# Moving one transpose of a fused attention and SwiGLU kernel from the tensor engine to the DMA engines

## The chip, the core and the metric

The kernel runs on one core of a Trainium2 chip. The metric is the device time of one execution in microseconds (us). One first run of the kernel before took 747.17 us. A profile's span is one execution as the trace sees it and is 1.5 to 1.8 us shorter than the time.

In profile lines, PE is the matrix engine (PEld its weight loads), DVE the vector engine, ACT the scalar engine, POOL and SP the two engines that issue the DMAs looked at here. SPq is SP's DMA queue: its time is that which one issue holds the queue. A DMA has landed when its data are complete for whoever waits; the time to landing counts from the start of its issue. A bracket such as [0.77 <-PE ps L441] gives how long the engine was idle before, and what ended that. `L466` is a line of that kernel's own file. Line numbers shift between kernels, so the text says what each one is.

## The reference, cut to what matters

```python
# attention, window of 64 keys, causal; B = H = 8, S = 576, D = 64
scores = where(0 <= i - j < 64, q @ k.T / 8, -1e9)
attn   = softmax(scores) @ v
x = attn.transpose(0, 2, 1, 3).reshape(4608, 512)
# feed-forward
g   = x @ w_gate;  val = x @ w_val            # 512 -> 1536
out = (g * sigmoid(g) * val) @ w_out          # 1536 -> 512, float32
```

## The kernel before

The 4608 tokens are 36 chunks of 128, and nine groups of four chunks. Attention works by chunk: `T` transposes q and k on PE, `Sx` makes scores, `AV` the weighted sum of v. DVE normalises that into `xb` (128 tokens x 512 features, bf16), in two halves. The feed-forward needs x with the features on the partitions, so `X` transposes `xb` into a quarter of `xT`. `F` then works on a whole group (512 columns of `xT`), `O` on one chunk of the group before. A helper records each operation with what it reads and writes; each engine runs its list in order and waits on semaphores.

```python
    def load_v(self, n):
        ...                                   # POOL: va <- v, cast to bf16
        g.op("sp", lambda e: e.dma_start(vb[64:128], va[0:64]), reads=lo, writes=[("vb", i, 1)], dma=True)
        if n + 1 < NCH:
            ...
            g.op("sp", lambda e: e.dma_start(vb2[0:64], va[64:128]), reads=hi, writes=[("vb", i2, 0)], dma=True)

    def T(self, n):
        ...                                   # PE: 4 transposes of kn, 4 of qn, into one PSUM bank
        g.op("dve", lambda e: e.tensor_copy(kd, tb[:, 0]), reads=[bk], writes=[("kT", n, p) for p in range(4)] + [(bk, "k")])
        g.op("act", lambda e: e.activation(qz[0:64, :, 0, :], tb[0:64, 1], ACTF.Copy),
             reads=[bk, (bk, "k")], writes=[("qz", iz, p, 0) for p in range(4)])
        g.op("dve", lambda e: e.tensor_copy(qz[64:128, :, 1, :], tb[64:128, 1]), reads=[bk], writes=[...])

    def X(self, n, eng="dve"):
        ...
        def pe(e):
            for c in range(4):
                r = e.transpose(tb[:, c, :], xb[:, 128 * c:128 * c + 128], self.ident[:, :])
            return r
        g.op("pe", pe, reads=["ident", ("xb", ix, 0), ("xb", ix, 1)], writes=[bk])
        ...
            g.op("dve", lambda e: e.tensor_copy(xo, tb), reads=[bk], writes=[("xT", it, u)])

    def F(self, c, f):
        ...
        xk = [("xT", it, u) for u in range(4)]          # all four quarters
        g.op("pe", mm(G, self.Wg), reads=xk + [("Wg", f)], writes=[gk])
        ...

    # the steady part of build()
        for c in range(1, NFC):                          # groups
            for u in range(4):
                n = 4 * c + u + 4                        # the chunk whose attention runs beside group c
                live = n < NCH
                load(n + 4)
                self.F(c, 3 * u)
                if live:
                    self.AV(n, 0)
                    if n + 1 < NCH:
                        self.Sx(n + 1, 0)
                self.F(c, 3 * u + 1)
                if live:
                    self.AV(n, 1)
                    if n + 1 < NCH:
                        self.Sx(n + 1, 1)
                if c > 1:
                    self.O(c - 1, u)
                if live and c > 1:
                    self.X(n)
                self.F(c, 3 * u + 2)
                ...
                if n + 2 < NCH:
                    self.T(n + 2)
```

The softmax here doesn't subtract the row's maximum and nothing guards it: scores larger than these inputs give would overflow.

Of the kernel before, what the change touches and what calls it, by code (L numbers as in the profile page):

```python
# [10 lines left out]
NCH = T // 128  # L11
# [138 lines left out]
class _Kernel:  # L150
# [165 lines left out]
            else:  # L316
                g.op("dve", lambda e, d=d, a=a: e.tensor_copy(d, a), reads=[bk], writes=zk)

    def load_v(self, n):
        g = self.g  # L320
        i = n % self.NV
        va = self.va[i]
        parts = list(self.segs(128 * n, 128))
        for j, (r, b, s, L) in enumerate(parts):
            d = va[r:r + L, :, 0:64]
            a = self.v[b, :, s:s + L, :].rearrange("h p d -> p h d")
            ks = [("va", i, j)] if len(parts) > 1 else [("va", i, 0), ("va", i, 1)]
            g.op("pool", lambda e, d=d, a=a: e.dma_start(d, a), writes=ks, dma=True)  # L328
        vb = self.vb[i]
        lo = [("va", i, 0), ("va", i)]  # L330
        hi = [("va", i, 0 if len(parts) == 1 else 1), ("va", i)]
        g.op("sp", lambda e: e.dma_start(vb[64:128], va[0:64]), reads=lo, writes=[("vb", i, 1)], dma=True)
        if n + 1 < NCH:
            i2 = (n + 1) % self.NV
            vb2 = self.vb[i2]
            g.op("sp", lambda e: e.dma_start(vb2[0:64], va[64:128]), reads=hi, writes=[("vb", i2, 0)], dma=True)
# [95 lines left out]
    def X(self, n, eng="dve"):  # L432
# [16 lines left out]
        else:  # L449
            g.op("act", lambda e: e.activation(xo, tb, ACTF.Copy), reads=[bk], writes=[("xT", it, u)])  # L450

    def F(self, c, f):
        g = self.g
        it, ih = c % self.NX, c % self.NH
        xT, hT = self.xT[it], self.hT[ih]
        i = self.n_s % self.NS
        self.n_s += 1
        sig, uu = self.sig[i], self.uu[i]
        xk = [("xT", it, u) for u in range(4)]
        G, gk = self.bank("f")  # L460
        V, vk = self.bank("f")

        def mm(bank, W):
            def pe(e):
                for kk in range(NK):
                    r = e.matmul(bank[:, :], W[:, kk, f * 128:f * 128 + 128], xT[:, kk, :],  # L466
                                 start=(kk == 0), stop=(kk == NK - 1))
                return r
            return pe

        g.op("pe", mm(G, self.Wg), reads=xk + [("Wg", f)], writes=[gk])
        g.op("act", lambda e: e.activation(sig[:, :], G[:, :], ACTF.Tanh, scale=0.5), reads=[gk], writes=[("sig", i)])  # L472
        g.op("pe", mm(V, self.Wv), reads=xk + [("Wv", f)], writes=[vk])
        g.op("dve", lambda e: e.scalar_tensor_tensor(uu[:, :], sig[:, :], 1.0, G[:, :], ALU.add, ALU.mult),  # L474
             reads=[("sig", i), gk], writes=[("uu", i)])
        g.op("dve", lambda e: e.scalar_tensor_tensor(hT[:, f, :], uu[:, :], 0.5, V[:, :], ALU.mult, ALU.mult),  # L476
             reads=[("uu", i), vk], writes=[("hT", ih, f)])
# [28 lines left out]
    def build(self):  # L506
        W = lambda a, b: (self.load_w("g", a, b), self.load_w("v", a, b))

        def load(n):
            if n < NCH:  # L510
                self.load_qk(n)
                self.load_v(n)

        self.first_loads()
        self.init()
        self.load_v(0)
        self.init_pool_a()
        self.load_v(1)
        self.init_pool_b()
        self.load_v(2)  # L520
        self.load_v(3)
        W(0, 1)
        W(1, 2)
        for f in range(2, 12, 2):
            W(f, f + 2)

        self.banks("a", [5, 6, 7, 4, 0, 1, 2, 3])
        self.first_casts(0)
        self.init_pt()
        self.first_T(0)  # L530
        self.first_T(1)
        self.first_casts(1)
        self.init_nmask()
        self.Sx(0, 0, True)
        self.Sx(1, 0, True)
        self.first_T(2)
        self.Sx(2, 0, True)
        self.first_T(3)
        self.Sx(3, 0, True)
        for n in range(4):  # L540
            self.Sx(n, 1, True)
            self.AV(n, 0)
        for n in range(4):
            self.AV(n, 1)
            if n > 0:
                self.X(n - 1, "act")
        self.X(3, "act")
        self.banks("a", [5, 6, 7])
        self.init_va(4)
        load(4)  # L550
        load(5)
        self.load_wo(0, 6)
        self.load_wo(6, 12)

        for f in range(6):
            self.F(0, f)
        self.T(4)
        self.F(0, 6)
        self.Sx(4, 0)
        self.F(0, 7)  # L560
        self.Sx(4, 1)
        self.T(5)
        load(6)
        self.F(0, 8)
        self.AV(4, 0)
        self.Sx(5, 0)
        self.F(0, 9)
        self.AV(4, 1)
        self.Sx(5, 1)
        load(7)  # L570
        self.F(0, 10)
        self.X(4)
        self.AV(5, 0)
        self.F(0, 11)
        self.AV(5, 1)
        self.T(6)
        load(8)
        self.O(0, 0)
        self.X(5)
        self.Sx(6, 0)  # L580
        self.T(7)
        load(9)
        self.Sx(6, 1)
        self.O(0, 1)
        self.AV(6, 0)
        self.Sx(7, 0)
        self.AV(6, 1)
        self.Sx(7, 1)
        self.T(8)
        self.O(0, 2)  # L590
        self.X(6)
        self.AV(7, 0)
        self.Sx(8, 0)
        self.AV(7, 1)
        self.Sx(8, 1)
        self.T(9)
        self.O(0, 3)
        self.X(7)
        load(10)
        load(11)  # L600
        for c in range(1, NFC):
            for u in range(4):
                n = 4 * c + u + 4
                live = n < NCH
                load(n + 4)
                self.F(c, 3 * u)
                if live:
                    self.AV(n, 0)
# [4 lines that stand above are left out]
                    self.AV(n, 1)  # L613
                    if n + 1 < NCH:
                        self.Sx(n + 1, 1)
                if c > 1:
                    self.O(c - 1, u)
                if live and c > 1:
                    self.X(n)
                self.F(c, 3 * u + 2)  # L620
                if live and c == 1:
                    self.X(n)
                if n + 2 < NCH:
                    self.T(n + 2)
        self.banks("o", [0, 1, 2, 3])
        for u in range(4):
            self.O(NFC - 1, u)
        self.g.emit()
# [42 lines left out]
```

## Time and profile before

| | |
|---|---|
| time | 376.6 us |
| PE busy, 160 to 220 us | 59.76 of 60 us |
| one chunk in the steady part | 9.64 us |
| `X` of one chunk, time that it holds PE | 0.22 us |
| `X` on DVE (one copy) | 0.42 us |

The busy line of the page of the kernel before: busy us, share of the span, instructions.

```profile
PE 352.3 (94%) x2624; PEld 192.0 (51%) x2624; DVE 254.6 (68%) x550; ACT 152.3 (41%) x260; POOL 107.5 (29%) x136
```

The chain of waits of the kernel before, over one chunk, without the short pieces of `AV`: start, us, what. L489 is `O`, L441 `X`, L466 `F`, L360 `T`, L389 `Sx`.

```profile
200.17 2.59 PE ps L489 x12
202.76 0.22 PE ps L441 x4
202.98 1.73 PE ps L466 x8
204.71 0.45 PE ps L360 x8
205.16 1.73 PE ps L466 x8
...
207.13 0.28 PE ps L389 x4
207.41 1.73 PE ps L466 x8
...
209.41 0.40 PE ps L389 x4
```

The next `O` begins at 209.81. All but 0.03 us of it is PE's, so what shortens PE's list shortens the kernel. `X` is 0.22 us of 9.64. Note also that `Sx`, the same four matmuls, takes 0.28 us once and 0.40 us once; this comes back below.

What the DVE and PE timelines of the kernel before show at the end of a chunk: the second half of `xb` (L429), the copy of `X` (L448), and `T` (L360).

```profile
211.13 0.43 DVE L429 TENSOR_TENSOR xb<-ps,rc 128x256 bf16<-128x256 f32 x1
212.66 0.42 DVE L448 COPY xT<-ps 128x512 bf16<-128x512 bf16 x1 [0.77 <-PE ps L441]
214.18 0.39 PE L360 MATMUL ps<-ident,kn 128*128 128x128 bf16 x4
```

Between `xb` complete (211.56) and the first `F` of the next chunk (214.63) lie 3.07 us, and 2.85 us once `X` is gone from PE. For the last chunk of a group that is the room which a slower transpose has (2.6 us at the last group, where no `T` runs).

The windows view of the kernel before: window, length, busy us of PE, PEld, DVE, ACT and POOL (with instructions), PE's clock, DMA share (over 1 where packets queue), GB/s.

```profile
205.20:211.50 6.30, 6.27 (x49) 3.39 (x48) 5.42 (x13) 2.86 (x5) 2.63 (x3) 1.00 1.05 79
211.50:214.00 2.50, 2.50 (x17) 1.23 (x15) 0.81 (x3) 1.08 (x2) 0.00 (x0) 1.00 0.08 22
```

The loads of q, k and v keep the DMA engines occupied for about 6 of every 9.6 us. Just when `xb` is complete they are nearly idle (0.08).

### The profile page before, as it was taken

What the parts mean: (1) busy time and instruction counts of PE and PEld (TensorE: products, weight loads), DVE (VectorE), ACT (ScalarE), POOL (GpSimd) and SP (SyncE); (2) the same over time, 40 slices, a digit from 0 to 9 for tenths busy, and PEclk for the clock granted to TensorE, in tenths of its full rate; (3) what the DMA queues carried; (4) which work ended last, traced back from release to release, by engine and by line L of the source; (5) the groups of instructions that cost most, each with busy time, mean ns of one, the idle gap of its engine ahead of it and who ended that gap; (6) DMA issues with size and microseconds to landing.
All of it is one profiled execution on the core that took longest, in us unless ns stands there. A gap on an engine that the chain in (4) does not pass through costs nothing.

```text
span 375.1 us, 6635 instructions
## 1 busy us (share of the span) xinstructions
PE 352.3 (94%) x2624; PEld 192.0 (51%) x2624; DVE 254.6 (68%) x550; ACT 152.3 (41%) x260; POOL 107.5 (29%) x136
## 2 busy tenths in 40 slices
PE   1589999999899999999999999999999999999986
PEld 1564555555455555555555555555555555444432
DVE  6668876688867777777777777777777777655520
ACT  2553535435444444444444444444444444233311
POOL 8985525434222222322222222422220000000000
PEclk9999999999999999999999999999999999999999
DMA  9999999979957777777888787877771000010012
GB/s 236 202 201 175 204 173 205 169 47 91 84 71 85 86 86 87 82 88 87 90 87 89 78 94 86 86 83 77 78 82 37 30 29 30 28 58 28 28 38 104
DMA packets 126158, 35.61 MB, mean 95 GB/s; under 512 B 108272, under 2 KB 121520, under 8 KB 126128
## 3 DMA queue, kind: packets, MB, share of 16 engines
q0 software_dynamic: 113152, 17.83, 64.3%
q1 hardware_dynamic: 11920, 16.31, 13.5%
q10 hardware_dynamic: 1056, 1.05, 0.9%
q8 instruction: 21, 0.34, 0.4%
q14 instruction: 9, 0.07, 0.1%
HBM read 37.75 MB, written 9.44 MB: 126 GB/s over the span
## 4 chain that ended last, share of the span: by engine, by line
PE 81%; DVE 13%; ACT 3%; DMA 2%; issue 1%
PE ps L466 41%; PE ps L489 25%; PE ps L389 5%; DVE hT L476 4%; DVE uu L474 4%; PE ps L360 3%; PE ps L441 2%; PE ps L420 2%; PE ps L419 2%; DVE xb L429 2%; DMA f<-in_q_dram 2%; ACT sig L472 1%; DVE pt L407 1%; ACT qz L366 1%; PE ps L302 1%
## 5 line engine op out<-in xcount | busy, mean ns | idle before, releaser
L474 DVE SCALAR_TENSOR_TENSOR uu<-sig,ps 128x512 bf16<-128x512 bf16 x108 | 74.1, 686 | 65.1 <-ACT sig L472 65.1
L466 PE MATMUL ps<-xT,Wg 128*128 128x512 bf16 x432 | 111.0, 380 | 2.4 <-DVE xT L448 1.7
L466 PE MATMUL ps<-xT,Wv 128*128 128x512 bf16 x432 | 110.9, 379 | 0.0
L489 PE MATMUL ps<-Wo,hT 128*128 128x512 bf16 x432 | 98.7, 380 | 2.1 <-DVE hT L476 2.1
L472 ACT ACTIVATE sig<-ps 128x512 bf16<-128x512 f32 x108 | 64.0, 592 | 43.4 <-PE ps L466 43.4
L277 POOL DMA_DIRECT2D qn<-in_q_dram x36 | 30.4, 847 | 164.2 <-PE ps L360 161.3
L476 DVE SCALAR_TENSOR_TENSOR hT<-uu,ps 128x512 bf16<-128x512 bf16 x108 | 74.2, 687 | 3.7
L466 PEld LDWEIGHTS ps<-xT,Wv 128*128 128x128 bf16 x432 | 42.2, 98 | 51.0
L489 PEld LDWEIGHTS ps<-Wo,hT 128*128 128x128 bf16 x432 | 40.9, 98 | 46.9 <-DVE hT L476 2.7
L401 ACT ACTIVATE pt<-ps 128x512 bf16<-128x512 f32 x72 | 42.9, 596 | 33.2 <-PE ps L389 30.5
L466 PEld LDWEIGHTS ps<-xT,Wg 128*128 128x128 bf16 x432 | 38.2, 98 | 32.6 <-DVE xT L448 2.0
L494 ACT ACTIVATE ost<-ps 128x512 f32<-128x512 f32 x36 | 21.5, 597 | 74.8 <-PE ps L489 74.8
L366 ACT ACTIVATE qz<-ps 64x512 bf16<-64x512 bf16 x32 | 18.9, 590 | 57.8 <-DVE kT L365 57.8
L328 POOL DMA_DIRECT2D va<-in_v_dram x40 | 34.7, 875 | 1.3 <-DVE wup L226 0.8
L389 PE MATMUL ps<-qz,kT 128*128 128x128 bf16 x288 | 30.8, 225 | 2.0 <-ACT qz L366 0.4
L429 DVE TENSOR_TENSOR xb<-ps,rc 128x256 bf16<-128x256 f32 x72 | 30.6, 425 | 2.5
L277 POOL DMA_DIRECT2D kn<-in_k_dram x36 | 30.7, 858 | 1.2 <-DMA Wv<-in_moe_w_val_dram 0.8
L448 DVE COPY xT<-ps 128x512 bf16<-128x512 bf16 x32 | 13.6, 423 | 24.1 <-PE ps L441 24.1
L407 DVE TENSOR_TENSOR pt<-pt,mask 128x512 bf16<-128x512 bf16 x64 | 26.6, 416 | 1.5 <-ACT pt L401 1.4
L419 PE MATMUL ps<-vb,pt 128*128 128x65 bf16 x288 | 26.9, 194 | 0.1
L420 PE MATMUL ps<-va,pt 128*128 128x65 bf16 x288 | 27.0, 194 | 0.0
L419 PEld LDWEIGHTS ps<-vb,pt 128*128 128x128 bf16 x288 | 22.6, 98 | 7.3 <-DVE xT L448 0.2
(44 smaller groups left out, 198.6 us busy)
## 6 DMA issues: line engine op xcount, KB each, us to landing
out_dram<-ost SPq DMA_DIRECT2D x36, 256.0 KB, 2.0
vb<-va SPq DMA_DIRECT2D x71, 80.0 KB, 2.1
va<-in_v_dram POOLq DMA_DIRECT2D x32, 128.0 KB, 4.5
qn<-in_q_dram POOLq DMA_DIRECT2D x28, 128.0 KB, 3.4
kn<-in_k_dram POOLq DMA_DIRECT2D x28, 128.0 KB, 4.4
Wo<-in_moe_w_out_dram POOLq DMA_DIRECT2D x2, 768.0 KB, 19.2
Wg<-in_moe_w_gate_dram POOLq DMA_DIRECT2D x5, 256.0 KB, 12.7
Wv<-in_moe_w_val_dram POOLq DMA_DIRECT2D x5, 256.0 KB, 13.3
```

The lines of the kernel that those rows point to most:

```text
L277: self.g.op("pool", lambda e, d=d, a=a: e.dma_start(d, a), writes=ks, dma=True)
L328: g.op("pool", lambda e, d=d, a=a: e.dma_start(d, a), writes=ks, dma=True)
L389: r = e.matmul(sv[:, w, c], self.kT[:, pr, k0:k0 + 128], qz[:, pr, :, 64 * w:64 * w + 64], start=not bias, stop=True)
L401: g.op("act", lambda e: e.activation(po, si, ACTF.Exp, scale=SCALE), reads=[bk], writes=[pk])
L419: e.matmul(av[:, j, :], pt[:, h, 0:128], vb[:, h, 0:65], start=True, stop=False)
L420: r = e.matmul(av[:, j, :], pt[:, h, 64:192], va[:, h, 0:65], start=False, stop=True)
L429: g.op("dve", lambda e: e.tensor_tensor(xo, av[:, :, 0:64], rb, ALU.mult), reads=[bk, ("rc", ir)], writes=[("xb", ix, half)])
L466: r = e.matmul(bank[:, :], W[:, kk, f * 128:f * 128 + 128], xT[:, kk, :], start=(kk == 0), stop=(kk == NK - 1))
L472: g.op("act", lambda e: e.activation(sig[:, :], G[:, :], ACTF.Tanh, scale=0.5), reads=[gk], writes=[("sig", i)])
L474: g.op("dve", lambda e: e.scalar_tensor_tensor(uu[:, :], sig[:, :], 1.0, G[:, :], ALU.add, ALU.mult), reads=[("sig", i), gk], writes=[("uu ...
L476: g.op("dve", lambda e: e.scalar_tensor_tensor(hT[:, f, :], uu[:, :], 0.5, V[:, :], ALU.mult, ALU.mult), reads=[("uu", i), vk], writes=[(" ...
L489: r = e.matmul(OB[:, :], hT[:, f, 128 * u:128 * u + 128], self.Wo[:, f, :], start=(f == 0), stop=(f == NF - 1))
```

## The change

The intent is to take the four transposes of `X` off PE, which bounds the kernel, and the copy off DVE. From group 3 on (chunks 12 to 35, 24 of 36) one DMA from SBUF to SBUF transposes `xb` into `xT`. The copies `vb <- va`, on the same SP queue, move from the load to behind that transpose.

```diff
+    def XD(self, n):
+        ix, it, u = n % 4, (n // 4) % self.NX, n % 4
+        xb = self.xb[ix]
+        xo = self.xT[it][:, :, 128 * u:128 * u + 128]
+        self.g.op("sp", lambda e: e.dma_start_transpose(xo, xb[:, :]), reads=[("xb", ix, 0), ("xb", ix, 1)],
+                  writes=[("xT", it, u)], dma=True)
 ...                                     (load_v is split: the two vb copies become copy_v)
-                load(n + 4)
+                load(n + 4, False)
 ...
+                if live and c > 1:
+                    self.XD(n)
+                    if n + 3 < NCH:
+                        self.copy_v(n + 3)
                 if c > 1:
                     self.O(c - 1, u)
-                if live and c > 1:
-                    self.X(n)
```

More of the change, by code (lines that the diff above doesn't have):

```diff
@@ L317, in first_T, with load_v @@
                 g.op("dve", lambda e, d=d, a=a: e.tensor_copy(d, a), reads=[bk], writes=zk)
-    def load_v(self, n):
+    def load_v(self, n, copy=True):
         g = self.g
@@ L328, in load_v, with copy_v @@
             g.op("pool", lambda e, d=d, a=a: e.dma_start(d, a), writes=ks, dma=True)
+        if copy:
+            self.copy_v(n)
+    def copy_v(self, n):
+        g = self.g
+        i = n % self.NV
+        va = self.va[i]
+        parts = list(self.segs(128 * n, 128))
         vb = self.vb[i]
@@ L507, in build, with load @@
         W = lambda a, b: (self.load_w("g", a, b), self.load_w("v", a, b))
-        def load(n):
+        def load(n, copy=True):
             if n < NCH:
                 self.load_qk(n)
-                self.load_v(n)
+                self.load_v(n, copy)
         self.first_loads()
@@ L599, in build @@
         load(10)
-        load(11)
+        load(11, False)
         for c in range(1, NFC):
@@ L622, in build @@
                     self.X(n)
+                    self.copy_v(n + 3)
                 if n + 2 < NCH:
```

## The prediction

> **What bounds it now.** PE. The windows view gives 59.8 us of PE work in each 60 us from 100 to 280 us at full clock, and the chain of waits is 81% PE. One chunk of 128 tokens takes 9.64 us (in the chain O matmuls begin at 200.17, 209.81, 219.45). DVE is busy about 71% there. The DMA engines average 0.8 but unevenly: the half-microsecond windows show them nearly idle from 211 to 214 us, between the loads of two chunks.
>
> **What is removed.** X for chunks 12 to 35, 24 of 36: four PE transposes and one DVE copy each. They are pipelined: in the chain of waits the four hold PE for 0.22 us. PE's gain is at most 24 x 0.22 = 5.3 us, 1.4% of 376.6. So I nearly rule out 2% faster. DVE loses 10.2 us of copies, which do not hold PE.
>
> **What is added.** 24 DMA transposes of 128x512 bf16 on SP's queue. The vb copies move to behind the transpose of the chunk before; they are then issued about a chunk after their va load, and three chunks before AV reads them, off the critical path.
>
> **What is on the critical path.** Three of four transposes in a group have a chunk or more to land. The fourth does not: F of the next group reads all 512 columns of xT at once. In the timeline the second xb half of a chunk is written at 211.55 us; without X the next F after T would start about 214.4 us. The slack is about 2.85 us (2.6 us at the last boundary, which has no T). There are six such boundaries, into groups 3 to 8. All in excess stops PE.
>
> How long is issue to landing? The vb copies (80 KB counted both ways, SBUF to SBUF) land in 2.1 us. The Trainium skill, "VectorE: DVE Perf Modes", section "The three transpose paths", gives 1309 ns for one 128x128 DMA transpose; four in series would be 5.2 us. "DMA: Bandwidth & Descriptors", "Latency and other measured facts", gives 261 GB/s effective, which would make 128 KB take 0.5 us beyond the fixed 2 us. My estimate is 3.5 us, between these, as the engines are quiet then: a stall of about 0.65 us at each of six boundaries, 4 us in all. Net: -5.3 + 4 = about -1.3 us.
>
> **Prediction:** 375.0 us, 8 in 10 between 370.8 and 391. Chances: faster by over 2% 0.03, within 2% 0.62, slower by over 2% 0.35. The upper side is long because each microsecond of landing time beyond the slack costs 6 us: 5 us to land means about 384 us, 7 us means about 396.
>
> **What would show it.**
> - Chunk period for u = 0 to 2 from group 2 on: 9.42 us instead of 9.64.
> - At the six boundaries, PE idle before the first F matmul of a group, released by the DMA of xT: landing time less 2.85 us, about 0.65 us each. Under 0.2 us: the whole gain stays, about 371.3. Over 2 us: slower.
> - DMA issues: 24 of xT, landing in 3 to 4 us.
> - DVE 244 us busy, PE idle nowhere else.
>
> **What would make it wrong.** A transpose that runs one 128x128 block after another or holds the SP queue for long; loads of q and k slowed until T waits; vb copies landing late. Above 10 us to land, the third transpose of a group matters too, and the time passes 410 us.

## The result, and the profile after

The time after is 371.61 us (371.56 to 371.77, 4 runs), before 376.61 us. The ratio is 0.9869, 95% interval 0.985 to 0.9888. (A ratio here and below is the mean time of one kernel's runs over that of the other's of the same rounds, so it is not quite the ratio of the medians quoted. Executions over 1.5% slower than the fastest of the same kernel are left out of the means.) So the change gained 5.0 us, 1.3%: within 2%, as predicted, but three times the 1.6 us that the prediction expected (the sum in its text gives 1.3).

The busy line of the page of the kernel after (it holds fewer PE records than instructions ran, 2483 of 2528, so PE's sum is a little low):

```profile
PE 344.3 (93%) x2483; PEld 186.8 (51%) x2528; DVE 244.7 (66%) x526; ACT 152.3 (41%) x260; POOL 107.4 (29%) x136
```

DVE lost 9.9 us, as the 24 copies make out (24 x 0.42 = 10.1). SP's queue over one chunk of the kernel after, in order of time (L464 is the transpose, L340 and L344 are the vb copies, L511 is the output), and below it the second half of `xb` on DVE (L437):

```profile
199.64 1.20 SPq L464 DMA_TRANSPOSE xT<-xb  x1
200.89 0.59 SPq L340 DMA_DIRECT2D vb<-va  x1
201.52 0.60 SPq L344 DMA_DIRECT2D vb<-va  x1
202.16 0.59 SPq L511 DMA_DIRECT2D out_dram<-ost  x1
...
209.06 1.19 SPq L464 DMA_TRANSPOSE xT<-xb  x1
```

```profile
208.61 0.42 DVE L437 TENSOR_TENSOR xb<-ps,rc 128x256 bf16<-128x256 f32 x1
```

A chunk now takes 209.06 - 199.64 = 9.42 us, 0.22 less. The transpose is issued 0.03 us after `xb` is complete and holds SP's queue for 1.2 us. From the view of the tile `xT` in the kernel after, min, median and max of the 24:

```profile
L464 SPq DMA_TRANSPOSE xT<-xb x24: 1189/1196/1281, 105.0 to 320.7; - x24
DMA to landing us min/median/max: 2.3/2.3/2.4
```

Every transpose lands 2.3 to 2.4 us after its issue begins, so about 2.35 us after `xb`, against a room of 2.85. The `xb` of 208.61 is the last of its group, and the next group's first `F` (L481) begins 2.85 us after it is complete (209.03), about half a microsecond after the landing:

```profile
211.88 1.03 PE L481 MATMUL ps<-xT,Wg 128*128 128x512 bf16 x4
```

In PE's waits there is none for the DMA of `xT`. So nearly all of 24 x 0.22 = 5.3 us stays: the time fell by 5.0 us, the profile's span by 5.3 (375.1 to 369.8).

### The profile page after: what moved, and what is told of

Same layout as the page of the kernel before. It is cut to its first block, busy times and chain, and to the rows that moved or that the text cites. A ratio compares the mean times of both kernels' runs of the same rounds, so it can differ in the third digit from the quotient of the medians.

```text
span 369.8 us, 6409 instructions
## 1 busy us (share of the span) xinstructions
PE 344.3 (93%) x2483; PEld 186.8 (51%) x2528; DVE 244.7 (66%) x526; ACT 152.3 (41%) x260; POOL 107.4 (29%) x136
## 4 chain that ended last, share of the span: by engine, by line
PE 80%; DVE 13%; ACT 3%; issue 2%; DMA 2%
PE ps L481 42%; PE ps L504 25%; PE ps L397 5%; DVE hT L491 4%; DVE uu L489 4%; PE ps L368 3%; PE ps L428 2%; PE ps L427 2%; DVE xb L437 2%; DMA f<-in_q_dram 2%; ACT sig L487 1%; DVE pt L415 1%; ACT qz L374 1%; PE ps L302 1%; PE ps L396 1%
## 5 line engine op out<-in xcount | busy, mean ns | idle before, releaser
L481 PE MATMUL ps<-xT,Wg 128*128 128x512 bf16 x408 | 108.1, 379 | 3.8 <-DVE xT L456 1.7
L481 PE MATMUL ps<-xT,Wv 128*128 128x512 bf16 x423 | 109.2, 379 | 0.5
L504 PE MATMUL ps<-Wo,hT 128*128 128x512 bf16 x420 | 96.4, 379 | 2.9 <-DVE hT L491 1.3
L487 ACT ACTIVATE sig<-ps 128x512 bf16<-128x512 f32 x108 | 64.0, 592 | 38.0 <-PE ps L481 38.0
L481 PEld LDWEIGHTS ps<-xT,Wv 128*128 128x128 bf16 x432 | 42.3, 98 | 51.0
L504 PEld LDWEIGHTS ps<-Wo,hT 128*128 128x128 bf16 x432 | 40.9, 98 | 46.8 <-DVE hT L491 2.7
L481 PEld LDWEIGHTS ps<-xT,Wg 128*128 128x128 bf16 x432 | 39.3, 98 | 38.3 <-DVE xT L456 2.0
L397 PE MATMUL ps<-qz,kT 128*128 128x128 bf16 x288 | 30.9, 224 | 2.0 <-ACT qz L374 0.4
L437 DVE TENSOR_TENSOR xb<-ps,rc 128x256 bf16<-128x256 f32 x72 | 30.6, 425 | 2.5
L428 PEld LDWEIGHTS ps<-va,pt 128*128 128x128 bf16 x288 | 20.2, 98 | 7.1
```

The source lines that it names most:

```text
L397: r = e.matmul(sv[:, w, c], self.kT[:, pr, k0:k0 + 128], qz[:, pr, :, 64 * w:64 * w + 64], start=not bias, stop=True)
L428: r = e.matmul(av[:, j, :], pt[:, h, 64:192], va[:, h, 0:65], start=False, stop=True)
L437: g.op("dve", lambda e: e.tensor_tensor(xo, av[:, :, 0:64], rb, ALU.mult), reads=[bk, ("rc", ir)], writes=[("xb", ix, half)])
L481: r = e.matmul(bank[:, :], W[:, kk, f * 128:f * 128 + 128], xT[:, kk, :], start=(kk == 0), stop=(kk == NK - 1))
L487: g.op("act", lambda e: e.activation(sig[:, :], G[:, :], ACTF.Tanh, scale=0.5), reads=[gk], writes=[("sig", i)])
L504: r = e.matmul(OB[:, :], hT[:, f, 128 * u:128 * u + 128], self.Wo[:, f, :], start=(f == 0), stop=(f == NF - 1))
```

## The experiments

The theory: the gain is PE's time in `X`; the landing time of the fourth transpose of each group is set against 2.85 us, only the excess counts, six times, and here there is none. The rivals: the gain comes from the moved copies, or from DVE and PSUM; or the transposes have plenty of room.

### 1. The moved copies alone

The kernel after with `X` back on PE.

```diff
-                    self.XD(n)
                     if n + 3 < NCH:
                         self.copy_v(n + 3)
                 if c > 1:
                     self.O(c - 1, u)
+                if live and c > 1:
+                    self.X(n)
```

> The kernel before, with only the move of the vb copies; X stays on PE behind O as before. Theory (the whole gain is the 24 x 0.22 us of PE time of the transposes): no change, 376.6 us, within 0.3. Rival (SP freed of its waits for va, or quieter DMA, gives part of the gain): below 375.

376.73 us against 376.69, ratio 1.0002 (0.9987 to 1.0017). The move alone gives nothing.

### 2. The transposes without the move

```diff
-                load(n + 4, False)
+                load(n + 4)
 ...
-                    if n + 3 < NCH:
-                        self.copy_v(n + 3)
```

> The change without the move: the vb copies stay in load, ahead of the transpose on SP's queue. In the trace of before the va load ends about 0.5 us before xb is ready, and two copies take 1.2 us of SP to issue. Theory (slack of 0.5 us between a landing of 2.3 us and 2.85 us): the transposes start about 0.8 us late, six stalls of 0.3 to 0.5 us, 373 to 375 us. Rival (the move is of no use): 371.6. If va lands later than that, more: up to 380.

372.47 us, ratio 0.9892 (0.9876 to 0.9909). The loss, 0.86 us against 371.61, is near the low end, but the mechanism expected was not there: POOL's loads run about two chunks ahead of the program's order, so the copies did not wait for va. They went out right behind the previous output DMA, long before the next transpose. Instead two of the six boundary transposes landed late, after 3.8 and 2.9 us, the rest after 2.3 to 2.5; the chain of waits of this kernel names both:

```profile
284.10 3.83 DMA xT<-xb
321.17 2.92 DMA xT<-xb
```

PE waited 1.1 us for these two. Why just these two were late was not settled. In both, the output DMA follows with no copies between, but so it does at three others that landed in time. Single late landings occur in other kernels too (4.1 us twice in experiment 5, 3.9 in 7, 4.3 in 11, 3.8 in 12), all of them on chunks that are not the last of a group, where they cost nothing. So 2.3 us is the usual time and no bound. With the transposes in place, what the move buys is 0.86 us; the transposes give the rest.

### 3. All transposes late

```diff
+                if c > 1:
+                    self.O(c - 1, u)
                 if live and c > 1:
                     self.XD(n)
                     if n + 3 < NCH:
                         self.copy_v(n + 3)
-                if c > 1:
-                    self.O(c - 1, u)
```

> Every transpose is issued behind the output DMA of O instead of ahead of it, so SP waits for ACT's copy of O and starts the transpose about 1.9 us later. Theory (landing 2.3 us against 2.85 us of slack, only excess counts, six times): stalls of about 1.4 us at six boundaries, 8.4 us, so 380 us. Rival (transposes have room in plenty): 371.6.

379.35 us, ratio 1.0072 (1.0057 to 1.0087): 7.7 us above the change, 2.7 above the kernel before. From this kernel's waits of PE (us in total, times, longest) and its timeline of PE at one boundary (L481 is `F`):

```profile
PE ps L481 <- DMA xT<-xb: 8.2, 6, 1.7
```

```profile
213.96 0.39 PE L368 MATMUL ps<-ident,qn 128*128 128x128 bf16 x4
215.65 1.04 PE L481 MATMUL ps<-xT,Wg 128*128 128x512 bf16 x4 [1.30 <-DMA xT<-xb]
```

There are six waits, as counted, of 1.4 us on average. The landing is again 2.4 us; only the issue was late. The room is small: the change works by where the transpose stands in SP's list.

### 4. Late, but for the last of a group

```diff
-                if live and c > 1:
+                if live and c > 1 and u == 3:
                     self.XD(n)
 ...                                     (then O, then XD and copy_v for u < 3)
```

> As the run with all late, but the fourth transpose of each group is early as in the change; 18 of 24 are late. Theory (only the fourth of a group is near the critical path): 371.6 us, within 0.3. Rival (late transposes cost by colliding with the loads, whichever they are): three quarters of the loss of the run with all late, about 378.

371.63 us, ratio 0.9866 (0.9852 to 0.9881), equal to the change. Eighteen late transposes cost nothing, so the loss of experiment 3 lies in the six last ones of a group alone.

### 5. PE's transposes put back

The change, and PE also does the four transposes again into a bank that nobody reads. There is no DVE copy.

```diff
                 if c > 1:
                     self.O(c - 1, u)
+                if live and c > 1:
+                    self.XP(n)          # X without its copy
```

> The change, and in addition PE does its four transposes of each chunk 12 to 35 again, into a PSUM bank that nobody reads; the DVE copy stays away. Theory (the gain is PE's time in X and nothing else): 24 x 0.22 us come back, 376.9 us. Rival (it was the DVE copy or its PSUM bank that was saved): 371.6 to 373.

376.94 us, ratio 1.0016 (1.0001 to 1.0031). That is 5.33 us above the change, against 24 x 0.22 = 5.3. This settles the source of the gain: PE's time, not the copy. The PSUM bank is in use again as well, but PE's waits show none that the change lacks, and the chain of waits of this kernel has the four transposes (L475) at their old price:

```profile
202.81 0.22 PE ps L475 x4
```

### 6. Four pieces of 128x128

```diff
-        self.g.op("sp", lambda e: e.dma_start_transpose(xo, xb[:, :]), reads=[("xb", ix, 0), ("xb", ix, 1)], ...
+        for k in range(4):
+            self.g.op("sp", lambda e, k=k: e.dma_start_transpose(xo[:, k, :], xb[:, 128 * k:128 * k + 128]),
+                      reads=[("xb", ix, k // 2)], ...
```

> Each transpose of 128x512 is cut into four of 128x128, all correct data. Theory A (the landing is mostly a fixed time, the 128x512 takes 1.2 us of SP to issue, and a 128x128 takes some 0.45 us of it): the last piece lands about 1.8 + 1.5 = 3.3 us after xb, stalls of 0.4 us, about 374 us. Theory B (the 1.2 us of issue is per transpose whatever its size): 4.8 us of issue, the last piece lands about 5.9 us after xb, stalls of 3 us, about 390 us. What the prediction feared (blocks one after another at 1.3 us each) would show as landings of a 128x128 near 1.3 us below that of 128x512 divided by four, which the 2.3 us of the change already speaks against.

379.77 us, ratio 1.0074 (1.0044 to 1.0105). From the view of the transpose's line in this kernel:

```profile
L465 SPq DMA_TRANSPOSE xT<-xb x96: 1093/1223/3151, 102.9 to 328.8; - x96
DMA to landing us min/median/max: 2.2/2.4/5.0
```

A quarter of the data holds SP's queue as long (1.22 us at the median) and lands no sooner (2.2 us at least, 2.4 at the median). The issue is theory B's. The time is better than its 390 us, because I let the first two pieces start with the first half of `xb`; at one boundary the pieces were issued from 209.95 on, the last at 213.69, and it landed at 216.03, 3.9 us after `xb` was complete (212.12) and not 5.9. So the 2.3 us of the change are a time per DMA, and the blocks do not add up within one.

### 7. k by DMA as well

The change, and k of chunks 15 to 35 goes by DMA from `kn` straight into `kT`; `T` keeps q (`TQ`).

```diff
                         self.copy_v(n + 3)
+                        self.XK(n + 3)     # dma_start_transpose(kT columns, kn)
 ...
-                    self.T(n + 2)
+                    (self.TQ if n + 2 >= 15 else self.T)(n + 2)
```

> The change, and k of chunks 15 to 35 is also transposed by DMA, from kn straight into kT, three chunks ahead; T keeps only q. It takes four more PE transposes (0.22 us) and one DVE copy out of 21 chunks. Theory (PE time is all that counts while the landing has room): 371.6 - 21 x 0.22 = 367.0 us. Rival (DMA or SP's queue saturates: two transposes of 1.2 us a chunk): 369 or more, with longer landings.

374.15 us, ratio 0.9937 (0.9922 to 0.9952). This missed badly: 7 us above the theory and 2.5 above the change. It was not the DMA: xT still landed in 2.3 us at the median, k in 2.6. The chain of waits of this kernel over part of a chunk (L527 is `O`, L504 `F`, L510 sig, L512 and L514 the two DVE steps of `F`, L486 and L487 the copies of q on DVE and ACT):

```profile
220.62 0.88 PE ps L504 x4
...
222.87 0.69 DVE hT L514
...
223.57 0.44 DVE qz L486
...
224.03 0.59 ACT qz L487
224.62 0.49 ACT sig L510
```

And PE's weight loads of `Sx`, once in its timeline and in its waits (us in total, times, longest):

```profile
224.68 0.23 PEld L397 LDWEIGHTS ps<-qz,kT 128*128 128x128 bf16 x4 [0.26 <-ACT qz L487]
PEld ps L397 <- ACT qz L487: 5.4, 21, 0.3
```

PE is no longer the whole chain. In writing `TQ` I had kept a dependence of `T`, that ACT's copy comes after a DVE copy; with k gone, that meant DVE's copy of q, which waits behind `F`'s two steps. ACT, and with it the sigmoid of the next `F`, then ran late, and a chunk took 9.52 us.

### 8. k and q by DMA

As 7, and q goes by DMA into a tile of its own; DVE and ACT copy from there.

```diff
+                        self.XQ(n + 3)     # dma_start_transpose(qt, qn)
 ...
-                    self.T(n + 2)
+                    (self.TZ if n + 2 >= 15 else self.T)(n + 2)   # TZ: copies qt -> qz, no PE
```

> As k by DMA, and q of the same chunks by DMA into a tile of its own, from which DVE and ACT copy into qz; PE does no transposes for these chunks. Theory: 371.6 - 42 x 0.22 = 362.3 us, if a third transpose in a row on SP does no harm. Rival (saturation of SP or of the DMA engines): above 366, with longer landings of xT, q or k.

362.80 us, ratio 0.964 (0.962 to 0.966). The number is as expected, but it is two misses that cancel. A chunk took 8.70 us, 0.72 less than in the change and not 0.45; and PE waited 5.9 us for xT at three boundaries. PE's wait, and the issues by kind in this kernel with their number and the median us to landing:

```profile
PE ps L519 <- DMA xT<-xb: 5.9, 3, 2.2
xT<-xb SPq DMA_TRANSPOSE x24, 3.8
kT<-kn SPq DMA_TRANSPOSE x21, 4.2
qt<-qn SPq DMA_TRANSPOSE x21, 4.0
```

The 13 transposes of xT from 114 to 226 us landed in 3.6 to 6.1 us, the next six, near the last loads, in 2.3 to 3.3, and from 286 us on, with no loads, all in 2.3 us. SP's and POOL's timelines of this kernel show why: the loads now start when q's transpose frees its buffer, and run into the next transpose of x.

```profile
196.15 0.88 POOL L278 DMA_DIRECT2D qn<-in_q_dram  x1 [6.76 <-DMA qt<-qn]
197.01 0.89 POOL L278 DMA_DIRECT2D kn<-in_k_dram  x1
197.36 1.20 SPq L465 DMA_TRANSPOSE xT<-xb  x1
```

### 9. k and q in another order

The edit is shown against experiment 8.

```diff
                     self.XD(n)
                     if n + 3 < NCH:
+                        self.XQ(n + 3)
                         self.copy_v(n + 3)
-                        self.XK(n + 3)
-                        self.XQ(n + 3)
+                    if n + 4 < NCH:
+                        self.XK(n + 4)
```

> k and q by DMA again, 21 chunks, but the transpose of q follows at once behind that of x, and that of k of one chunk further comes last. In the run before, xT took 4 to 6 us to land while the loads of q, k and v were under way, and PE waited for it 5.9 us at three boundaries; the loads start when the transpose of q frees its buffer. Theory (landing is 2.3 us when the DMA engines are quiet, and the loads' phase decides that): loads start about 1.3 us after xT's transpose has ended instead of running into it, the stalls go, 362.8 - 5.9 = about 357 us. Rival (three transposes a chunk are too much for the queue however ordered): 361 or more.

362.54 us (361.03 to 364.82), ratio 0.962 (0.9604 to 0.9636): hardly better. Three of the six runs had a clock of 0.995; the three at full clock took 361.03 to 362.70, against 362.32 to 364.11 in experiment 8. In the profiled run, the slowest (364.82), PE still waited 6.2 us for xT, in four places, and xT took 3.2 us at the median. The rival's number (361 or more) held. The loads did start earlier against x, but q's and k's transposes and the loads together still reached into the next transpose of x. Whether some other order of three fits was not tried.

### 10. The loads together with the transpose

The change; only the loads of chunks 16 to 35 are held until `xb` is written. The work is the same.

```diff
                     self.XD(n)
                     if n + 3 < NCH:
                         self.copy_v(n + 3)
+                    if n + 4 < NCH:
+                        self.load_qk(n + 4, [("xb", n % 4, 0), ("xb", n % 4, 1)])   # an added read
+                        self.load_v(n + 4, False)
```

> The change, with only the loads of q, k and v of chunks 16 to 35 held until xb is written, so that they run together with the transpose of x. Same work, other time. Theory (2.3 us to land needs quiet DMA engines): xT lands in 4 to 6 us, five boundaries stall by 1.2 to 3.2 us, 378 to 388 us. Rival (landing is 2.3 us whatever runs beside it): 371.6 us.

374.38 us, ratio 0.9943 (0.9922 to 0.9963), 2.8 us above the change. The 20 transposes issued beside loads landed in 3.3 to 4.6 us, the last four, with none, in 2.3 to 2.5. From this kernel's issues and PE's waits:

```profile
xT<-xb SPq DMA_TRANSPOSE x24, 3.5
```

```profile
PE ps L481 <- DMA xT<-xb: 4.2, 5, 1.7
```

The profiled run was the slowest (375.37). The direction is the theory's and the rival (2.3 us whatever runs beside it) is out; my size was too large. The loads met only the end of the transpose: of the one issued at 219.87, the windows view shows the packets moving from about 221.0 to 221.7, as late after the issue as in the change, and the next packets, of loads and vb copies, only from about 221.9 on; it landed at 223.5. So what grew is the time between a transpose's own packets and its landing; why is not shown.

### 11. As 7, ACT no longer behind DVE

The edit is shown against experiment 7.

```diff
-        ... tensor_copy(qz[64:128, :, 1, :], tb[64:128]), ... writes=[("qz", iz, p, 1) ...] + [(bk, "k")])
+        ... tensor_copy(qz[64:128, :, 1, :], tb[64:128]), ... writes=[("qz", iz, p, 1) ...])
 ...
-             reads=[bk, (bk, "k")], writes=[("qz", iz, p, 0) for p in range(4)])
+             reads=[bk], writes=[("qz", iz, p, 0) for p in range(4)])
```

> k by DMA as in the run that missed (374.15 us), but ACT's copy of q's half no longer waits for DVE's copy of the other half (a dependence that I had put in when cutting k out of T). In that run S waited for ACT's copy, which ended 0.26 us late. Theory (the missing gain went into this wait): 371.6 - 21 x 0.22 = 367.0 us, within 1.5. Rival (two transposes on the queue cost it): 373 to 374 again.

361.69 us, ratio 0.9603 (0.9589 to 0.9617). The dependence was the whole loss of run 7, and more: 12.5 us lie between the two. The time is also 5.3 us better than PE's removed work explains. A chunk takes 8.92 us, 0.50 less than in the change, of which 0.22 is k's share of `T`. The weight loads of `Sx` (L397 in both kernels) waiting for DVE, first in the kernel after (in all, and once in its timeline), then in this one:

```profile
PEld ps L397 <- DVE xb L437: 4.7, 28, 0.4
206.88 0.23 PEld L397 LDWEIGHTS ps<-qz,kT 128*128 128x128 bf16 x4 [0.16 <-DVE xb L437]
```

```profile
PEld ps L397 <- DVE xb L437: 1.3, 6, 0.4
```

`Sx` takes 0.28 and 0.40 us in the chain of the kernel after, as it did before, and 0.22 both times in this one:

```profile
208.86 0.22 PE ps L397 x4
```

So about 0.24 us of each chunk that counts as PE's went beyond the 0.22 us that `Sx` needs. For 0.18 us of it, in the longer `Sx`, the trace names DVE's work on `xb`, which still read PSUM; these waits fell by 3.4 us in all. For the 0.06 us of the shorter one it names nothing. There ACT's copy of q ended 0.11 us before the weight loads in the kernel after and 1.2 us before in this one, so q's copy is likely, but not shown. Run 11 both moved k and freed ACT; what freeing ACT would give without moving k was not run. So how the 0.28 us beyond k's share (0.50 less 0.22) split between the two is open.

### 12. Begun one group earlier

As 11, with x of chunks 8 to 10 and k from chunk 11 on by DMA too; the vb copies there also move ahead of the last `F` of the chunk.

```diff
-                if live and c > 1:
-                    self.XD(n)
+                if live:
+                    if c > 1 or u < 3:
+                        self.XD(n)
 ...
-                    (self.TQ if n + 2 >= 15 else self.T)(n + 2)
+                    (self.TQ if n + 2 >= 11 else self.T)(n + 2)
```

> The best so far (x and k by DMA, ACT's copy of q free of DVE's, 361.69 us), begun one group earlier: x of chunks 8 to 10 and k from chunk 11 on go by DMA too; x of chunk 11 stays on PE, because it would have too little slack ahead of its group. Each k transpose moved took 0.50 us from a chunk there (9.42 to 8.92 us), each x transpose 0.22: 361.7 - 4 x 0.50 - 3 x 0.22 = 359.0 us. Against it: the first 80 us have the DMA engines full of weights, so landings can be long and the gain half of that; above 361.5 would mean that the early transposes harm.

358.18 us (357.05 to 358.32, 5 rounds), ratio 0.951 (0.9497 to 0.9523). This is 0.8 us below what was expected and 13.4 us faster than the change; it is the best kernel. PE never waits for the DMA of xT or kT. The busy line of its page:

```profile
PE 333.9 (94%) x2416; PEld 177.4 (50%) x2416; DVE 235.1 (66%) x498; ACT 155.1 (44%) x260; POOL 107.4 (30%) x136
```

## Why the prediction was right or wrong

- **What bounds it, and the gain at most: right.** PE's list was the chain. The prediction took 24 x 0.22 = 5.3 us as the most to be had; the change gained 5.0, and putting only PE's transposes back cost 5.33.
- **Where the risk lies: right.** It named the fourth transpose of a group, a room of 2.85 us and six boundaries. Runs 3 and 4 show just that: six waits, 8.2 us in all, for a loss of 7.7 us, and nothing when only the other 18 were late.
- **The landing time: wrong, and this is the step that failed.** "My estimate is 3.5 us, between these, as the engines are quiet then: a stall of about 0.65 us at each of six boundaries, 4 us in all." It landed in 2.3 us, the stall was zero, and the term of +4 us in the sum is 0. The prediction itself said what follows: "the whole gain stays, about 371.3"; it was 371.61.
- **Why the estimate was too long.** It was put between two estimates worked out from figures of the Trainium skill, 5.2 and 2.5 us: 1309 ns for one 128x128 DMA transpose, times four ("VectorE: DVE Perf Modes", section "The three transpose paths"), and 0.5 us from a rate, plus 2 us ("DMA: Bandwidth & Descriptors", section "Latency and other measured facts"). Run 6 shows that multiplying was wrong: a 128x128 transpose and a 128x512 one both hold the queue 1.2 us, and land in 2.4 and 2.3 us at the median. The nearest thing in the trace was better evidence, the vb copies, SBUF to SBUF, that landed in 2.1 us (80 KB moved once, not counted both ways). I read that number and then moved away from it.
- **What was right about quiet engines.** 2.3 us holds because the DMA engines are idle then, but for the single late landings named under experiment 2. In run 10 the same transpose beside loads took 3.5 us, in run 8, with two more transposes a chunk as well, 13 of the 24 took 3.6 to 6.1. The Trainium skill says that DMAs from all engines "will ultimately run on the same 16 DMA engines and interleave with each other" ("DMA: Bandwidth & Descriptors", section "Issuing engines are not separate DMA queues"); run 10 agrees in that loads issued by POOL lengthened the landing of a transpose issued by SP.
- **The copies: right that they stay off the critical path.** Alone the move changes nothing (run 1). That it helps the transposes the prediction did not say: without it the change loses 0.86 us (run 2), with two late landings whose cause is open.
- **PE full by its busy time: incomplete.** The prediction read "59.8 us of PE work in each 60 us" as no wait left. PE showed 59.76 busy of 60 us, yet a chunk could lose 0.28 us beyond the removed work (run 11), some of it waits inside this busy time. The Trainium skill warns that matmul busy time "is a bad metric for how close a kernel is to roofline, because matmuls are pipelined" ("Trainium Kernel Development and Optimization", section "Performance Expectations"); this trace agrees. It did not touch this prediction: with `X` gone `Sx` still took 0.28 and 0.40 us.

## What to carry to other kernels

When work moves from the bounding engine to a slower path, its gain is the time it held that engine in the chain of waits, and its cost is only the excess of its latency over the room at the step that ends last; take that latency from the nearest DMA in the trace rather than from a figure multiplied by size. The room is made by the order of the queue and by when the other DMAs run, so put the transfer ahead of what waits for something else, and where loads leave the DMA engines quiet. And before cutting more from a full engine, look at the dependences that its other work passes through: one needless order between two copies turned a gain of 10 us into a loss of 2.5.

## What the Trainium skill lacked or had wrong

- "VectorE: DVE Perf Modes", section "The three transpose paths", gives 1309 ns for a 128x128 DMA transpose and nothing on other sizes or on the queue. Here a 128x128 and a 128x512 transpose from SBUF to SBUF each held SP's queue for 1.2 us. The 128x512 one landed in 2.3 to 2.4 us with quiet DMA engines, the 128x128 one in 2.2 us at least and 2.4 at the median.
- "DMA: Bandwidth & Descriptors", section "Latency and other measured facts", gives a rate for transposes (261 GB/s) but no time to landing. For 128 KB the latency decided: 2.3 us, where the rate alone gives an estimate of 0.5. With the fixed cost of about 2 us that the page states for DMAs (fitted on DMAs issued from GpSimd, not SP) the estimate is 2.5, near the 2.3 measured.
- The same page, section "Rules for kernel authors", says that a transpose next to ordinary DMAs "needs nothing". All such runs here were correct, but no page tells what it costs: the landing grew from 2.3 us to 3.5 (run 10, at the median) and to 3.6 to 6.1 (13 transposes of run 8, which has two more transposes a chunk as well).
